# Identity products into spare columns of the y bank, behind the first FFN product

## Chip, cores and metric

One core of a Trainium2 chip runs the whole kernel in one launch. The metric is the device time of that launch in microseconds; the kernel before takes 502.52 us, the median of three runs (502.21 to 503.4).

## What is computed

A gated linear attention with a decay for each channel, and a feed-forward block on its output:

```python
for t in range(S):                                   # B, H, S, D = 4, 8, 768, 48
    state = alpha[:, :, t, :, None] * state + np.einsum('bhd,bhe->bhde', k[:, :, t], v[:, :, t])
    y[:, :, t] = np.einsum('bhd,bhde->bhe', q[:, :, t], state)
x = y.transpose(0, 2, 1, 3).reshape(B * S, H * D)    # 3072 x 384
h = x @ w_in                                         # 384 x 2048
out = (0.5 * h * (1.0 + erf(h / sqrt(2)))) @ w_out   # 2048 x 384
```

## The kernel before

The 3072 tokens are cut into 12 groups of 256 (`g`), and the eight heads of a group into two units (`u`), so there are 24 units; unit n is group n // 2. A unit passes through these steps:

- VectorE (DVE) scans the decays (L283, L304) and multiplies queries and keys by them (L299, L309).
- TensorE (PE) forms the `scores` (L325) into a PSUM tile `s`. DVE masks them into `ss` (L340), and ScalarE (ACT) copies the turned keys out of the same tile into `kn` (L334, `turned_out`).
- PE multiplies the masked scores with v (`inside`, L399) into `ybank`, and `kn` with v into the same tile (`sums`, L426; in the first two groups `running`, L367). DVE adds the sums up to the states (L454, `chain`), and PE adds the share of the earlier chunks to y (`outside_part`, L487).
- y is split into a high and a low part for the FFN: ACT casts y to the high part (L541, `x_high`), PE subtracts that from y in the bank (L550, `x_minus`), and ACT casts what is left to the low part (L556, `x_rest`). Some rows are then moved between partitions by DMAs that SP and ACT issue (L564, `spread`).

The FFN runs in steps (g, f) over eight pairs of 128 columns of `w_in`: 18 products of 256 columns into the PSUM tile `hp` (L572, `gemm1`), two Gelus on ACT (L593, L594), the low part by a subtraction (L603 on PE and L607 on ACT early on, L599 on DVE later), and 12 products into `acc` (L622, `gemm2`). The weights come as 64-bit floats and are turned into two 32-bit parts on DVE and ACT (L197 to L259) in the first 135 us, while the first groups are already being worked on.

`ybank` is one PSUM tile of two banks with 512 columns each. Columns 0 to 255 of a bank hold y and columns 256 to 447 hold the sums; columns 448 to 511 hold nothing.

The order on PE, DVE, ACT and SP is made in Python before anything is issued. A planner gives each step an assumed cost (`COST`, us) and a start; the steps sorted by planned start are then issued one by one under a manual schedule, so the planned start sets the order on each engine. What a step must wait for is found by the framework from what was issued before it, and is expressed as a semaphore count that the other engine has to reach.

Into planned gaps of PE before the first `gemm1` the plan puts `busy(n)`: n products of the identity with itself (L1080) into `spare`, a tile that nobody reads. A gap gives int((gap - 0.3) / 0.24) of them. A float32 product is two matmul instructions in the profile (42 rows for 21 products).

Of the kernel before, what the change touches and what calls it, by code (L numbers as in the profile page):

```python
# [25 lines left out]
WAIT = 0.15  # L26
SLOW = 1.1
FILL = 0.24
UNTIL = 60.0
SUMS = 2  # L30
LANES = 8
# [13 lines left out]
def gla_then_gelu_ffn(ctx: ExitStack, tc: tile.TileContext, q, k, v, alpha, akq, w_in, w_out, out):  # L45
    nc = tc.nc
    B, H, D, S = q.shape
# [3 lines left out]
    C = 128  # L51
# [24 lines left out]
    ident = const.tile([P, P], F32, name="ident")  # L76
# [20 lines left out]
    minus = const.tile([P, P], F32R, name="minus")  # L97
# [55 lines left out]
    ybank = ps_y.tile([P, 2, BANK], F32, name="ybank")  # L153
# [448 lines left out]
    def gelu_rest(g, f, hp, ghi):  # L602
        nc.tensor.matmul(hp, lhsT=minus, rhs=ghi, start=False, stop=True, skip_group_check=True)  # L603

        def out():
            glo = half_tile("glo", LO_GAP, g, f)
            nc.scalar.copy(glo, hp)  # L607
            return glo

        return out  # L610
# [313 lines left out]
    steps, plan, evacuated = [], [], set()  # L924
# [42 lines left out]
    def gemm1_op(g, t):  # L967
# [18 lines left out]

        if g < NSB and t < UNTIL:
            st["minus"] = Op("PE", "minus", lambda: st.update(rest=gelu_rest(g, f, st["hp"], st["gh"])), [st["gelu"]], rank=-3)
# [41 lines left out]
    def choose(e, t):  # L1030
        best = None
        for o in waiting[e]:
            at = when(o)
            if at is not None and at <= t + 1e-9 and (best is None or (o.rank, o.n) < (best.rank, best.n)):
                best = o
        if e != "PE":
            return best
        if best is not None and not (best.late and best.at() + MARGIN > t):
            return best
        held = best  # L1040
        second = [s for s in steps if s["gemm2"].start is None]
        if second:
            at = when(second[0]["gemm2"])
            if at is not None and at <= t + 1e-9:
                return second[0]["gemm2"]
        if len(second) < 2:
            hp_free = steps[-2]["low"].end if len(steps) > 1 else 0.0
            if hp_free is not None and hp_free + WAIT <= t + 1e-9 or len(steps) < 2:
                g = next_step(t)
                if g is not None:  # L1050
                    return gemm1_op(g, t)
        return held
# [3 lines left out]
    while True:  # L1056
        moved = False
        for e in ("DVE", "ACT", "PE", "SP", "POOL"):
            if free_at[e] <= t + 1e-9:
                o = choose(e, t)  # L1060
# [13 lines left out]
    plan.append(Op("DVE", "part", lambda: last["out"](), [last["gemm2"]]))  # L1074
    plan[-1].start = t + 10
    spare = ps_h.tile([P, 2, G], F32, tag="hp", name="spare")[:, 0, :P]

    def busy(n):
        for _ in range(n):
            nc.tensor.matmul(spare, lhsT=ident, rhs=ident, start=True, stop=True)  # L1080

    first = min(o.start for o in plan if o.name == "gemm1")
    early = sorted((o for o in plan if o.eng == "PE" and o.start <= first), key=lambda o: o.start)
    for o, after in zip(early, early[1:]):
        n = int((after.start - o.end - 0.3) / FILL)
        if n > 0:
            plan.append(Op("PE", "minus", lambda n=n: busy(n)))
            plan[-1].start = o.start + 0.01
    plan.sort(key=lambda o: (o.start, o.n))

# [72 lines left out]
```

## Time and profile before

| what | value |
|---|---|
| median of three runs (lowest, highest) | 502.52 us (502.21, 503.4) |
| profiled execution, its own time | 503.02 us |
| its span, first to last instruction | 501.0 us |
| PE busy / weight loads | 487.1 us (97%) / 474.9 us (95%) |
| DVE busy | 301.7 us (60%) |
| ACT busy | 217.9 us (43%) |
| mean granted TensorE clock | 0.995 |

The profiled execution took 2.02 us more than its span, and 0.50 us more than the median of the runs. Busy shares are means over the span: DVE is busy nearly without a break in the first 135 us and a quarter of the time behind that.

### The profile page before, as it was taken

What the parts mean: (1) busy time and instruction counts of PE and PEld (TensorE: products, weight loads), DVE (VectorE), ACT (ScalarE), POOL (GpSimd) and SP (SyncE); (2) the same over time, 40 slices, a digit from 0 to 9 for tenths busy, and PEclk for the clock granted to TensorE, in tenths of its full rate; (3) what the DMA queues carried; (4) which work ended last, traced back from release to release, by engine and by line L of the source; (5) the groups of instructions that cost most, each with busy time, mean ns of one, the idle gap of its engine ahead of it and who ended that gap; (6) DMA issues with size and microseconds to landing.
All of it is one profiled execution on the core that took longest, in us unless ns stands there. A gap on an engine that the chain in (4) does not pass through costs nothing.

```text
span 501.0 us, 13833 instructions
## 1 busy us (share of the span) xinstructions
PE 487.1 (97%) x5970; PEld 474.9 (95%) x5970; DVE 301.7 (60%) x580; ACT 217.9 (43%) x467; POOL 34.8 (7%) x69
## 2 busy tenths in 40 slices
PE   7898999999999999999999999999999999999996
PEld 7777899999998999998999999999999999999996
DVE  6999999999789999899266264251232211211211
ACT  2776856645445555555352352351332222222221
POOL 4100011000111121211010011000000000000000
PEclk9998999999999999999999999999999999999999
DMA  8967363531024453344031020010010000000001
GB/s 299 391 189 236 123 234 128 188 128 65 0 89 147 139 170 120 103 163 143 1 86 60 2 82 2 0 49 2 1 46 4 0 33 1 33 0 1 33 0 37
DMA packets 17153, 44.20 MB, mean 88 GB/s; under 512 B 2240, under 2 KB 8512, under 8 KB 17088
## 3 DMA queue, kind: packets, MB, share of 16 engines
q1 hardware_dynamic: 16656, 42.87, 25.3%
q8 instruction: 49, 0.80, 0.7%
q10 hardware_dynamic: 432, 0.39, 0.3%
q14 instruction: 16, 0.13, 0.1%
HBM read 36.18 MB, written 4.72 MB: 82 GB/s over the span
## 4 chain that ended last, share of the span: by engine, by line
PE 85%; DVE 9%; issue 2%; ACT 1%; DMA 1%; SPq 0%; DVEq 0%
PE acc L622 38%; PE hp L572 38%; PE s L325 3%; PE ybank L399 2%; PE ybank L487 2%; DVE rp L304 2%; DVE pp L283 2%; PE ybank L426 2%; DMA akq<-in_akq_dram 1%; DVE qk L299 1%; DVE ss L340 1%; DVE x L545 1%; DVE glo L599 1%; DVE akq L309 0%; DVE states L454 0%
## 5 line engine op out<-in xcount | busy, mean ns | idle before, releaser
L572 PE MATMUL hp<-x,wih 128*128 128x256 f32 x1152 | 202.5, 278 | 0.0
L572 PEld LDWEIGHTS hp<-x,wih 128*128 128x128 f32 x1152 | 179.2, 189 | 0.6
L572 PE MATMUL hp<-x,wil 128*128 128x256 f32 x576 | 159.8, 278 | 0.0
L599 DVE TENSOR_TENSOR glo<-hp,ghi 128x512 fp32r<-128x512 f32 x92 | 63.1, 686 | 160.4 <-ACT hp L594 160.3
L593 ACT ACTIVATE ghi<-hp 128x512 fp32r<-128x512 f32 x96 | 57.4, 598 | 197.7 <-PE hp L572 197.4
L622 PE MATMUL acc<-woh,ghi 128*128 128x384 f32 x384 | 130.9, 341 | 0.0
L622 PE MATMUL acc<-wol,ghi 128*128 128x384 f32 x384 | 128.9, 336 | 0.0
L572 PEld LDWEIGHTS hp<-x,wil 128*128 128x128 f32 x576 | 108.9, 189 | 0.0
L622 PE MATMUL acc<-woh,glo 128*128 128x384 f32 x384 | 82.5, 335 | 2.0 <-DVE glo L599 2.0
L622 PEld LDWEIGHTS acc<-woh,ghi 128*128 128x128 f32 x384 | 72.1, 188 | 1.7
L622 PEld LDWEIGHTS acc<-wol,ghi 128*128 128x128 f32 x384 | 72.1, 188 | 0.0
L622 PEld LDWEIGHTS acc<-woh,glo 128*128 128x128 f32 x384 | 67.8, 188 | 2.8 <-DVE glo L599 2.7
L594 ACT ACTIVATE hp<-hp 128x512 f32<-128x512 f32 x96 | 56.9, 593 | 0.0
L304 DVE TENSOR_TENSOR_SCAN rp<-akq,rp,top 128x255 f32<-128x255 f32 x48 | 35.8, 774 | 0.8
L283 DVE TENSOR_TENSOR_SCAN pp<-akq,top 128x256 f32<-128x256 f32 x48 | 31.0, 679 | 3.9 <-POOL qk L299 2.0
L299 POOL TENSOR_TENSOR qk<-akq,pp 128x512 f32<-128x512 f32 x18 | 24.8, 1380 | 45.8 <-DVE pp L283 15.5
L325 PE MATMUL s<-qk,akq 48*64 48x112 f32 x768 | 23.9, 260 | 2.3 <-DVE akq L309 1.1
L541 ACT CAST x<-ybank 64x256 fp32r<-64x256 f32 (+4 forms) x60 | 20.0, 333 | 9.4 <-PE ybank L487 5.0
L334 ACT COPY kn<-s 128x384 f32<-128x384 f32 x24 | 11.5, 480 | 28.9 <-DVE ss L340 16.3
L454 DVE TENSOR_TENSOR states<-ybank,states 128x96 f32<-128x96 f32 x66 | 16.8, 255 | 10.1 <-ACT x L541 7.8
L309 DVE TENSOR_TENSOR akq<-akq,rp 128x512 f32<-128x512 f32 x24 | 22.2, 926 | 0.7
L325 PEld LDWEIGHTS s<-qk,akq 48*64 48x64 f32 x768 | 19.3, 133 | 3.2 <-issue 1.5
(79 smaller groups left out, 390.3 us busy)
## 6 DMA issues: line engine op xcount, KB each, us to landing
akq<-in_akq_dram SPq DMA_DIRECT2D x22, 768.0 KB, 5.2
st<-in_moe_w_in_dram SPq DMA_DIRECT2D x8, 768.0 KB, 4.4
st<-in_moe_w_out_dram SPq DMA_DIRECT2D x8, 768.0 KB, 4.9
vn<-in_v_dram SPq DMA_DIRECT2D x12, 384.0 KB, 4.9
out_dram<-part SPq DMA_DIRECT2D x11, 384.0 KB, 3.0
x<-z SPq DMA_DIRECT2D x63, 32.0 KB, 1.9
akq<-in_akq_dram SPq DMA_DIRECT2D x2, 512.0 KB, 5.2
akq<-in_akq_dram SPq DMA_DIRECT2D x2, 256.0 KB, 4.5
```

The source lines that it names most:

```text
L283: nc.vector.tensor_tensor_scan(pp[:, i], at[:, i], top, MID, ALU.mult, ALU.min)
L299: eng.tensor_tensor(out=qs[:, :, :, :CS], in0=by_chunk(qt), in1=by_chunk(pp), op=ALU.mult)
L304: nc.vector.tensor_tensor_scan(rp[:, i, G - 2 :: -1], at[:, i, G - 1 : 0 : -1], top[:, 1:], rp[:, i, G - 1 :], ALU.mult, ALU.min)
L309: nc.vector.tensor_tensor(out=kt, in0=kt, in1=rp, op=ALU.mult)
L325: nc.tensor.matmul(d["s"][o, h, e : e + KW], lhsT=d["kt"][r, i, t], rhs=d["qs"][r, i, j], start=True, stop=True)
L454: d["chain"] = nc.vector.tensor_tensor(out=st[j + 1], in0=new, in1=st[j], op=ALU.add)
L541: nc.scalar.copy(hi, y)
L572: nc.tensor.matmul(hp[:, j, :], lhsT=a[:, j, i * P : (i + 1) * P], rhs=x[:, i, :], start=(j == 0 and i == 0 and n == 0), stop=(i == NK - 1 ...
L593: nc.scalar.activation(ghi, hp, AF.Gelu)
L594: nc.scalar.activation(hp, hp, AF.Gelu)
L599: nc.vector.tensor_tensor(out=glo, in0=hp, in1=ghi.bitcast(F32), op=ALU.subtract)
L622: nc.tensor.matmul(acc[t], lhsT=a[:, j, t * C : (t + 1) * C], rhs=w[:, j, :], start=(first and j == 0 and k == 0 and w is wo_hi[f]), stop= ...
```

## The change

Gaps of the plan are now filled up to a planned start of 80 us and no longer only up to the first `gemm1`. Behind the first `gemm1` a gap must leave 0.8 us over, in place of 0.3, and the products go into columns 448 to 511 of bank 1 of `ybank`, 64 columns wide and without the start flag, in place of `spare`, which shares its slots with `hp`.

```diff
+WARM_UNTIL, WARM_REST = 80.0, 0.8
...
     spare = ps_h.tile([P, 2, G], F32, tag="hp", name="spare")[:, 0, :P]
-
-    def busy(n):
+    margin = ybank[:, 1, 2 * C + 4 * D :]
+
+    def busy(n, to, anew):
         for _ in range(n):
-            nc.tensor.matmul(spare, lhsT=ident, rhs=ident, start=True, stop=True)
+            nc.tensor.matmul(
+                to, lhsT=ident, rhs=ident[:, : to.shape[1]], start=anew, stop=True, skip_group_check=not anew
+            )
 
     first = min(o.start for o in plan if o.name == "gemm1")
-    early = sorted((o for o in plan if o.eng == "PE" and o.start <= first), key=lambda o: o.start)
+    early = sorted((o for o in plan if o.eng == "PE" and o.start <= WARM_UNTIL), key=lambda o: o.start)
     for o, after in zip(early, early[1:]):
-        n = int((after.start - o.end - 0.3) / FILL)
+        anew = after.start <= first
+        n = int((after.start - o.end - (0.3 if anew else WARM_REST)) / FILL)
         if n > 0:
-            plan.append(Op("PE", "minus", lambda n=n: busy(n)))
+            plan.append(Op("PE", "minus", lambda n=n, anew=anew: busy(n, spare if anew else margin, anew)))
             plan[-1].start = o.start + 0.01
```

The whole program gains seven products, in two places; nothing else changes its order on any engine. Lines are numbered one higher in the changed kernel up to the fill, so L325 is L326 there.

The first place is PE between the scores of unit 4 (`s_0_709`) and `inside` of the same unit. Before:

```order
L550 MATMUL ybank<-z_695,minus 128x128 x2
L550 MATMUL ybank<-x_557,minus 128x128 x2
L325 MATMUL s_0_709<-qk_120,akq_117 64x112 x16
L399 MATMUL ybank<-ss_0_736,vn_116 64x64 x16
L426 MATMUL ybank<-vn_116,kn 64x48 x12
```

With the change:

```order
L551 MATMUL ybank<-z_695,minus 128x128 x2
L551 MATMUL ybank<-x_557,minus 128x128 x2
L326 MATMUL s_0_709<-qk_120,akq_117 64x112 x16
L1082 MATMUL ybank<-ident 128x64 x6
L400 MATMUL ybank<-ss_0_742,vn_116 64x64 x16
L427 MATMUL ybank<-vn_116,kn 64x48 x12
```

Six products stand between the scores and `inside`. They are issued before the casts of `x_rest` of unit 3, which the plan starts later than the scores. On ACT the order around these casts is the same as before (`z_695` and `x_557` are where unit 3's low part goes):

```order
L557 CAST z_695<-ybank 128x256 [waits PE_49]
L557 CAST x_557<-ybank 128x256
L565 DMA x_557<-z_695 16x512 [waits Activation_49]
L565 DMA x_557<-z_695 16x512 [waits DMAHW5_49]
L565 DMA x_557<-z_695 16x512 [waits DMAHW7_49,Activation_49]
L335 COPY kn<-s_0_709 128x384 [waits DVE_49]
```

The rows are the same; the count of PE's semaphore that the first cast waits for is not. Before it is 352, which PE reaches with the last subtraction of unit 3; the scores bring it to 368. In the changed program it is 374, which PE reaches with the sixth identity product.

The second place is PE between the subtractions of unit 4 and the Gelu subtraction of step (1, 0), with the change:

```order
L604 MATMUL hp_1_784<-ghi_1_831,minus 128x512
L551 MATMUL ybank<-x_856,minus 128x256 x2
L1082 MATMUL ybank<-ident 128x64
L604 MATMUL hp_0_835<-ghi_0_866,minus 128x512
```

One product stands there, and the `x_rest` cast of unit 4 waits for it in the same way.

## Rows read from the trace of the kernel before

**Rows 1.** The page, part 1 and the chain that ended last by engine.
```profile
PE 487.1 (97%) x5970; PEld 474.9 (95%) x5970; DVE 301.7 (60%) x580; ACT 217.9 (43%) x467; POOL 34.8 (7%) x69
...
PE 85%; DVE 9%; issue 2%; ACT 1%; DMA 1%; SPq 0%; DVEq 0%
```

**Rows 2.** Windows: stretch, length, busy us (count) of engines, PEclk, DMA share, GB/s.
```profile
20.00:25.00 5.00, 4.01 (x86) 3.56 (x86) 4.82 (x9) 2.78 (x10) 1.43 (x4) 1.00 0.99 364
45.00:50.00 5.00, 5.00 (x68) 4.71 (x62) 4.83 (x10) 3.57 (x8) 0.21 (x1) 0.66 0.60 190
60.00:500.00 440.00, 434.72 (x5087) 427.75 (x5087) 248.11 (x493) 181.32 (x389) 27.63 (x38) 1.00 0.20 65
```

**Rows 3.** The quarter of a microsecond in which the clock falls.
```profile
45.75:46.00 0.25, 0.25 (x3) 0.25 (x2) 0.25 (x1) 0.05 (x1) 0.00 (x0) 0.62 0.04 8
```

**Rows 4.** Timeline of PE: start, us, line, out<-in, shape, count [idle before <-releaser].
```profile
9.79 1.38 PE L1080 MATMUL spare<-ident 128*128 128x128 f32 x10
...
23.05 1.00 PE L325 MATMUL s<-qk,akq 48*64 48x112 f32 x32 [0.99 <-PE ybank L487]
...
41.96 1.00 PE L325 MATMUL s<-qk,akq 48*64 48x112 f32 x32
44.46 0.69 PE L399 MATMUL ybank<-ss,vn 64*64 64x64 f32 x32 [1.50 <-issue]
45.12 0.67 PE L426 MATMUL ybank<-vn,kn 64*64 64x48 f32 x24
45.72 0.74 PE L572 MATMUL hp<-x,wih 128*128 128x256 f32 x2
...
49.56 1.10 PE L487 MATMUL ybank<-qk,states 48*48 48x64 f32 x32
...
54.15 0.50 PE L603 MATMUL hp<-ghi,minus 128*128 128x512 f32 x1 [0.70 <-ACT hp L594]
...
56.67 1.00 PE L325 MATMUL s<-qk,akq 48*64 48x112 f32 x32
```

**Rows 5.** The chain that ended last, in order of time: start, us, what.
```profile
45.79 3.85 PE hp L572 x18
...
64.59 2.32 PE hp L572 x18
```

**Rows 6.** Timeline of ACT; ACTq is a DMA issue that holds ACT's queue.
```profile
42.07 0.37 ACT L556 CAST z<-ybank 128x256 fp32r<-128x256 f32 x1 [0.30 <-PE ybank L550]
42.34 0.38 ACT L556 CAST x<-ybank 128x256 fp32r<-128x256 f32 x1
42.47 2.07 ACTq L564 DMA_DIRECT2D x<-z  x3
44.59 0.48 ACT L334 COPY kn<-s 128x384 f32<-128x384 f32 x1 [1.87 <-DVE ss L340]
...
54.50 0.60 ACT L556 CAST x<-ybank 128x512 fp32r<-128x512 f32 x1
```

**Rows 7.** Timeline of PE's weight loads.
```profile
41.37 0.30 PEld L550 LDWEIGHTS ybank<-z,minus 128*128 128x128 f32 x2
41.59 0.30 PEld L550 LDWEIGHTS ybank<-x,minus 128*128 128x128 f32 x2
```

**Rows 8.** Timeline of DVE.
```profile
43.68 0.68 DVE L340 TENSOR_TENSOR ss<-s,mask 128x512 f32<-128x512 f32 x1
...
47.32 0.81 DVE L454 TENSOR_TENSOR states<-ybank,states 128x96 f32<-128x96 f32 x3
...
54.66 0.69 DVE L309 TENSOR_TENSOR akq<-akq,rp 128x512 f32<-128x512 f32 x1
```

**Rows 9.** Timeline of SP's queue.
```profile
42.47 1.78 SPq L564 DMA_DIRECT2D x<-z  x3
46.25 0.37 SPq L197 DMA_DIRECT2D st<-in_moe_w_in_dram  x1
```

**Rows 10.** The page, DMA issues: count, KB each, median us to landing.
```profile
x<-z SPq DMA_DIRECT2D x63, 32.0 KB, 1.9
```

## The prediction

> **What bounds the kernel now.** The page comes first: PE is busy 97% of the span and carries 85% of the chain that ended last, DVE 9% [rows 1]. So a microsecond that PE loses or gains is worth close to a microsecond, if nothing else holds PE later. The windows come next, read for PEclk. It is 1.00 (2.4 GHz) from 60 to 500 us, and 0.66 in the mean from 45 to 50 [rows 2]. At the two levels 1.00 and 0.50 a mean of 0.66 is 5 x 0.34 / 0.5 = 3.4 us at half clock, 1.2 GHz; the quarter from 45.75 has a mean between the levels, so the fall lies there [rows 3]. PE's timeline then tells what PE did before it: the scores of unit 4 start at 41.96 and end at 42.96, PE idles 1.50 us, and L399 and L426 run from 44.46 [rows 4]. An idle time of 0.99 us, at 22 to 23 us, left the clock at 1.00 [rows 4, 2]. The chain gives the price of the half clock: 18 products of L572 take 3.85 us there, and 2.32 where they stand at full clock behind the same kind of small products, 1.53 us less [rows 5].
>
> PE's idle time itself ends with DVE: the mask L340 starts at 43.68 and ends at 44.36, and L399 needs it [rows 8, 4].
>
> **The six products.** What does one cost? Each is two instructions with a full load of 128x128 weights. Ten instructions of L1080 with 128 moving columns take 1.38 us, 0.138 each with the last one's drain [rows 4]; that is the upper end. Half the columns might halve it, to 0.07, the lower end. But L550's weight loads come in pairs that start 0.22 us apart, 0.11 each [rows 7], though its 128 columns take one instruction and not two. There the load sets the pace, and 64 columns keep the same load, so I take 0.11: 12 x 0.11 = 1.32 us, from 42.96 to 44.28. By the ends it is 43.80 or 44.62. On PE alone this fits ahead of 44.46, or costs 0.16 us at the upper end.
>
> **The wait that they bring.** The products write bank 1 of `ybank`, and the low-part cast of unit 3 reads y from both banks. It is issued behind the products, and its semaphore count is now the one that the sixth product reaches (374 in place of 352). Before, it started at 42.07, right behind the subtraction [rows 6]; now it starts at 44.28, **2.21 us later** (1.73 to 2.55 by the ends above). Queued behind it on ACT, in order: the second cast (42.34, ends 42.72), three DMA issues that hold ACT from 42.47 to 44.54, and the copy of `kn`, which started at 44.59, right behind them [rows 6]. None has slack, as the copy was not waiting for the mask (44.36) but for the queue. So `kn` starts at 44.59 + 2.21 = 46.80.
>
> Who waits for that? L399 needs the second cast, since it overwrites y: 42.72 + 2.21 = 44.93, so it starts at about 45.0, 0.5 late. L426 needs `kn`: it started at 45.12, and starts at 47.33, after 1.6 us of new idle time. L572 follows at 47.93. The end of the scores to the start of L572 was 45.72 - 42.96 = 2.76 us, and becomes 4.97. **The gap that was to be filled is moved behind the products, not closed.**
>
> The Trainium skill (PSUM — Partial Sum Buffer, "PSUM bank collisions raise a hardware error") has a rule on this: two engines must not touch one bank in the same partitions at once, whichever columns they touch, so accesses are to be guarded by bank. By that rule the wait is due, and the time is the forecast below; were columns enough, no wait would be due, and the time would be the second rival's. No row of the kernel before shows it, as its scores go to another tile than y.
>
> **Other queues.** SP's three x<-z issues move from 42.47 to 44.68 and end at 46.46, so the weight fetch behind them moves from 46.25 by 0.2 [rows 9]; it serves a conversion some us later. The last x<-z issue of ACT ends at 46.75 and lands 1.9 later [rows 10], at 48.65; its reader, the first product of step (1, 0), stands behind L487 (49.56 to 50.6, and later now). Both are hidden. DVE's L454 starts at 47.32 and needs L426, so it waits until 47.93 and ends 0.6 us later than before; L487, which needs it, stood 1.4 us behind its end (48.13 against 49.56) [rows 8, 4]. So DVE's delay is hidden by PE's own. The **seventh product** stands ahead of L603, where PE idles 0.70 until 54.15 [rows 4]; it takes 0.22. The cast that now waits for it starts at 54.50 [rows 6], so it costs nothing; with that cover gone it would cost 0.22.
>
> **The sum.** L572 of step (0, 1) starts 2.21 us later. Whether the clock falls again then decides. I take it that it does: PE idles from about 44.3 to 45.0 and from 45.7 to 47.3, over 2 us in 3, where 1.50 us were enough before. The fall came 1.3 us after the idle time had ended (44.46 to 45.75); 1.3 after 47.33 is 48.6, with most of L572 still to come. It costs at most the 1.53 of before; part of the slow stretch may lie on L487, for which no row at half clock exists, and on its slack, so I bound it by 0.8 and 1.53 and take 1.2. Of the old fall, 1.53 goes. So +2.21 - 1.53 + 1.2 = +1.9 us, and the profiled execution's 503.02 becomes 504.9. It stood 0.50 above the median of the runs, so the forecast against that is **504.4 us**, 0.37% slower. Its own range: 1.73 - 1.53 + 0.8 = +1.0 to 2.55 - 1.53 + 1.53 = +2.55, 503.5 to 505.1; the 0.3 by which the lowest run of before lies under its median, added above, makes 505.4.
>
> **Rivals.**
> First, the clock stays at 1.00. For it: the products keep PE at work until 44.3, and each of the two idle times is not far above 0.99, which did no harm. Against it: they nearly touch. Then +2.21 - 1.53 = +0.7 us (0.2 to 1.0): 503.2. The Trainium skill (TensorE: Matmul & The Clock Gate, "Why this matters for your kernels") warns only of idle gaps longer than any of these; by its rule no fall would come, and none should have come in the kernel before, where rows 3 show one behind 1.50 us.
>
> Second, the fill works: the cast is not held, or its delay is hidden, the 1.50 us are filled, and the clock does not fall. It ends on the other side, faster. The price is not the whole 1.53: L487 can move up 1.4 until DVE's L454 holds it, and L325 at 56.67 stands 1.32 behind the end of DVE's L309 (55.35) [rows 4, 8], and DVE has no idle time there. So at most -1.27, 501.3. It decides if the cast starts before 42.5. The semaphore count speaks against it.
>
> Third, worse: the runs of before lie 1.19 us apart, and if the fall is missing in most of them, nothing comes back: +2.21 + 1.2 on 502.5 is 505.9. The Trainium skill (same page, "The HAM clock gate") says that the point at which the clock changes differs from run to run; no row here shows that.
>
> **Chances.** Clock falls again 0.62; clock stays 0.22; fill works 0.09; worse 0.07. A measurement of this kernel can tell 0.3% (1.5 us) from no change, so faster means under 501.0 and slower over 504.0. Faster: the lower third of the second rival, 0.03. Within: the rest of it 0.06, nearly all of the first 0.20, and 0.14 of the likeliest case, from its lower part: 0.40. Slower: the rest, 0.57. The range from 502.6 to 505.4 leaves out the second rival, most of the third, and little of the first at its lower end: under 0.2.
>
> **What would show it.** Right: six products in 1.2 to 1.5 us behind the scores, the cast of L557 at about 44.3, `kn` (L335) at about 46.8, L427 at about 47.3 behind a new idle time of PE with ACT as its releaser, and a stretch at 0.50 soon after. Wrong: the cast still at 42.1 and L427 at 45.1 (the count means something else), or PEclk at 1.00 from 45 to 55 (first rival), or products twice as fast as taken, which moves all by 0.5 us.

## The result, and the profile after

The change makes the kernel **slower by 0.71%**: 506.43 us in the median of 10 runs (505.23 to 507.8) against 503.01 for the kernel before in the same sessions (10 runs, 501.86 to 505.47), ratio 1.0071, 95% interval 1.0059 to 1.0083. The forecast was 504.4 with a range to 505.4: the right side, and too small. The profiled execution took 507.0 us with a span of 504.9, against 503.02 and 501.0 before.

The page first, busy time and the chain by engine, which answer to [rows 1]:

```profile
PE 490.5 (97%) x5984; PEld 478.1 (95%) x5984; DVE 302.1 (60%) x580; ACT 217.8 (43%) x467; POOL 35.1 (7%) x69
...
PE 87%; DVE 7%; issue 2%; ACT 2%; ACTq 1%; DMA 1%; SPq 0%; DVEq 0%
```

PE gains 14 instructions and 3.4 us of busy time, 1.5 us more than those 14 take (1.55 + 0.33 in the timeline below): other products have become slower. Where, the windows tell (columns as in [rows 2]):

```profile
45.00:50.00 5.00, 2.95 (x62) 2.72 (x63) 3.52 (x8) 3.06 (x8) 0.21 (x1) 0.66 0.34 74
50.00:55.00 5.00, 5.00 (x53) 4.70 (x53) 4.86 (x9) 2.59 (x6) 0.00 (x0) 0.66 0.75 283
60.00:500.00 440.00, 437.96 (x5137) 430.78 (x5136) 250.95 (x497) 183.77 (x394) 27.61 (x38) 1.00 0.20 64
```

From 45 to 50 us PE is busy for 2.95 us in place of 5.00 [rows 2]. Two neighbouring stretches now have a mean of 0.66, where before there was one: 2 x 5 x 0.34 / 0.5 = 6.8 us at 1.2 GHz, twice the 3.4 of before. PE's timeline over the same place, to be laid beside [rows 4]:

```profile
42.14 1.00 PE L326 MATMUL s<-qk,akq 48*64 48x112 f32 x32
43.07 1.55 PE L1082 MATMUL ybank<-ident 128*128 128x64 f32 x12
45.35 0.69 PE L400 MATMUL ybank<-ss,vn 64*64 64x64 f32 x32 [0.74 <-ACT x L557]
...
47.74 1.09 PE L427 MATMUL ybank<-vn,kn 64*64 64x48 f32 x24 [1.69 <-ACT kn L335]
...
52.90 1.31 PE L488 MATMUL ybank<-qk,states 48*48 48x64 f32 x32
...
56.84 0.33 PE L1082 MATMUL ybank<-ident 128*128 128x64 f32 x2
57.71 0.50 PE L604 MATMUL hp<-ghi,minus 128*128 128x512 f32 x1 [0.54 <-ACT hp L595]
...
60.25 1.00 PE L326 MATMUL s<-qk,akq 48*64 48x112 f32 x32
...
77.09 1.00 PE L326 MATMUL s<-qk,akq 48*64 48x112 f32 x32
```

The one idle time of 1.50 us has become two, 0.74 and 1.69 us, both ended by ACT. ACT's timeline says why; it answers to [rows 6]:

```profile
44.66 0.37 ACT L557 CAST z<-ybank 128x256 fp32r<-128x256 f32 x1 [2.70 <-PE ybank L1082]
44.92 0.38 ACT L557 CAST x<-ybank 128x256 fp32r<-128x256 f32 x1
45.06 2.11 ACTq L565 DMA_DIRECT2D x<-z  x3
47.21 0.48 ACT L335 COPY kn<-s 128x384 f32<-128x384 f32 x1 [1.91 <-DVE wol L260]
```

ACT idles 2.70 us before the cast, which the identity products release. The releaser printed for the copy of `kn` is a DVE instruction, but what stands right in front of it is the DMA issues that hold ACT's queue until 47.17. The chain that ended last prices the slow stretch, beside [rows 5]:

```profile
47.74 1.09 PE ybank L427 x24
48.83 4.14 PE hp L573 x18
52.97 1.24 PE ybank L488 x32
54.21 2.33 PE hp L573 x18
```

Of the trace alone, in the forecast's own terms (start times of the same instruction in both traces):

| term | forecast | measured |
|---|---|---|
| scores of unit 4 later (a difference of the two executions that arises ahead of the products) | 0 | +0.18 |
| cast held, so L427 later | +2.21 (1.73 to 2.55) | 47.74 - 45.12 - 0.18 = +2.44 |
| old fall of the clock goes | -1.53 | -1.53 |
| clock falls again | +1.2 (0.8 to 1.53) | L427 1.09 - 0.67, L573 4.14 - 2.32, L488 1.31 - 1.10: +2.45 |
| sum | +1.9 | +3.54 |

The scores of unit 5 start at 60.25 in place of 56.67, 3.58 us later, and those of unit 6 at 77.09 in place of 73.51, again 3.58. So the loss is complete at unit 5. Some 0.3 us more come much later, in two steps between 157 and 167 us and between 228 and 252 us; what makes them is left open.

### The profile page after: what moved, and what is told of

Its sections match the earlier page's. It is cut to its first block, busy times and chain, and to the rows that moved or that the text cites. A ratio compares the mean times of both kernels' runs of the same rounds, so it can differ in the third digit from the quotient of the medians.

```text
span 504.9 us, 13861 instructions
## 1 busy us (share of the span) xinstructions
PE 490.5 (97%) x5984; PEld 478.1 (95%) x5984; DVE 302.1 (60%) x580; ACT 217.8 (43%) x467; POOL 35.1 (7%) x69
## 4 chain that ended last, share of the span: by engine, by line
PE 87%; DVE 7%; issue 2%; ACT 2%; ACTq 1%; DMA 1%; SPq 0%; DVEq 0%
PE acc L623 38%; PE hp L573 38%; PE s L326 3%; PE ybank L488 2%; PE ybank L400 2%; PE ybank L427 2%; DVE rp L305 1%; DVE pp L284 1%; ACTq L565 1%; DMA akq<-in_akq_dram 1%; PE ybank L368 1%; DVE x L546 1%; DVE glo L600 1%; DVE ss L341 0%; DVE states L455 0%
## 5 line engine op out<-in xcount | busy, mean ns | idle before, releaser
L573 PE MATMUL hp<-x,wih 128*128 128x256 f32 x1152 | 203.1, 279 | 0.0
L573 PEld LDWEIGHTS hp<-x,wih 128*128 128x128 f32 x1152 | 179.4, 189 | 0.7
L573 PE MATMUL hp<-x,wil 128*128 128x256 f32 x576 | 160.1, 278 | 0.0
L573 PEld LDWEIGHTS hp<-x,wil 128*128 128x128 f32 x576 | 109.2, 190 | 0.0
L326 PE MATMUL s<-qk,akq 48*64 48x112 f32 x768 | 23.9, 260 | 1.3 <-PE ybank L488 0.9
L455 DVE TENSOR_TENSOR states<-ybank,states 128x96 f32<-128x96 f32 x66 | 16.8, 255 | 11.4 <-ACT x L542 7.8
L310 DVE TENSOR_TENSOR akq<-akq,rp 128x512 f32<-128x512 f32 x24 | 22.2, 927 | 0.7
L326 PEld LDWEIGHTS s<-qk,akq 48*64 48x64 f32 x768 | 19.3, 133 | 2.2 <-PE ybank L488 1.0
```

The costliest lines, as they stand in the source:

```text
L310: nc.vector.tensor_tensor(out=kt, in0=kt, in1=rp, op=ALU.mult)
L326: nc.tensor.matmul(d["s"][o, h, e : e + KW], lhsT=d["kt"][r, i, t], rhs=d["qs"][r, i, j], start=True, stop=True)
L455: d["chain"] = nc.vector.tensor_tensor(out=st[j + 1], in0=new, in1=st[j], op=ALU.add)
L573: nc.tensor.matmul(hp[:, j, :], lhsT=a[:, j, i * P : (i + 1) * P], rhs=x[:, i, :], start=(j == 0 and i == 0 and n == 0), stop=(i == NK - 1 ...
```

## Experiments

Each kernel ran in five rounds beside the kernel before; in these sessions that took 503.2, 503.14 and 503.17 us.

**1. The products behind the cast.** The same products go at the end of the gap and not at its start, so the cast is issued ahead of them.

```diff
-            plan[-1].start = o.start + 0.01
+            plan[-1].start = o.start + 0.01 if anew else after.start - 0.01
```

> The six products stay where they are on TensorE, but are issued behind the low-part cast instead of ahead of it, so that they wait for the cast and the cast does not wait for them. Theory A (the wait on the products holds ACT's queue, and all else follows): the cast starts near 42.1, the copy of kn near 44.6, the sums near 45.2, the idle time of 1.5 us is filled; the clock stays at 1.00 there, and the kernel is 0 to 1.3 us faster than before, some 4 us faster than the change. Theory B (the products themselves cost, by their place on TensorE or by writing that bank): slower than before by about as much as the change, +2 to +3.5 us.

Measured: 502.73 us (501.68 to 504.77, 12 runs), ratio 0.9988 (0.9976 to 0.9999). The profiled execution, PE's timeline, then ACT's, then the window:

```profile
42.60 1.55 PE L1082 MATMUL ybank<-ident 128*128 128x64 f32 x12
44.13 0.69 PE L400 MATMUL ybank<-ss,vn 64*64 64x64 f32 x32
44.82 0.67 PE L427 MATMUL ybank<-vn,kn 64*64 64x48 f32 x24
...
55.21 1.00 PE L326 MATMUL s<-qk,akq 48*64 48x112 f32 x32 [0.19 <-DVE akq L310]
...
74.23 0.47 PE L573 MATMUL hp<-x,wih 128*128 128x256 f32 x2 [1.24 <-issue]
```

```profile
41.78 0.37 ACT L557 CAST z<-ybank 128x256 fp32r<-128x256 f32 x1 [0.29 <-PE ybank L551]
```

```profile
45.00:50.00 5.00, 4.84 (x83) 4.51 (x80) 4.86 (x10) 4.49 (x10) 0.21 (x1) 1.00 0.69 198
```

The wait is gone with the order alone; number, shape and target of the products are those of the change. The 1.50 us are filled without a break, the clock stays at 1.00, and at the scores of unit 5 PE is 1.46 us ahead of the kernel before. Of these, 0.29 were there at the scores of unit 4 (41.67 against 41.96), ahead of the products; the other 1.17 are the gain, and DVE's L310 holds PE from more. At 74 us that gain is lost in one wait of 1.24 us. That became experiment 6.

**2. The same place, another bank.** The products stand where the change puts them, and write 64 spare columns of a tile of `acc`, widened to a whole bank (the lines that widen it are left out).

```diff
...
-            plan.append(Op("PE", "minus", lambda n=n, anew=anew: busy(n, spare if anew else margin, anew)))
+            plan.append(Op("PE", "minus", lambda n=n, anew=anew: busy(n, spare if anew else spare_cols[1][:, DM : DM + 64], anew)))
```

> Same place in the order as in the change, but the products go to spare columns of the second acc bank (its tile made 512 columns wide) instead of the y bank. Theory A: no cast reads that bank, so the first cast's count is 352 again and it starts near 42.1; time as in the run with the products behind the cast, 0 to 1.3 us faster than before. Theory B (the place in the order costs): as slow as the change, +3 us. If only the y bank's write costs, this one and the run before it differ by over 2 us.

Measured: 503.28 us (501.83 to 504.1, 12 runs), ratio 0.9994 (0.9982 to 1.0006). PE, then ACT:

```profile
42.49 1.55 PE L1084 MATMUL acc<-ident 128*128 128x64 f32 x12
```

```profile
41.67 0.37 ACT L557 CAST z<-ybank 128x256 fp32r<-128x256 f32 x1 [0.30 <-PE ybank L551]
```

The cast starts before the products. So neither their place nor their time holds it, but that they write the tile that it reads, though no column of it that it reads. Bank and tile change together here, so the run does not tell which of the two sets the wait. As in experiment 1 the lead, 1.57 us of which 0.40 were there ahead of the products, is lost at 74 us.

**3. One product in place of six**, in the first place alone.

```diff
+        if not anew:
+            n = 1 if n > 1 else 0
```

> One product in place of six at the first place, none at the second. Theory A: the cast waits for the scores (42.96) and the one product, so it starts near 43.4, 1.3 us late instead of 2.6, and kn and the sums move by the same 1.3; the clock falls as in both kernels, for once or twice 3.4 us. So slower than before by 1 to 2.5 us, with one sixth of the products. Theory B: the cost goes with the number of products: one sixth of 3.5, 0.6 us at most.

Measured: 505.09 us (502.76 to 506.08, 11 runs), ratio 1.0028 (1.0015 to 1.0042). PE's timeline, then the windows:

```profile
43.30 0.43 PE L1082 MATMUL ybank<-ident 128*128 128x64 f32 x2
44.87 0.88 PE L400 MATMUL ybank<-ss,vn 64*64 64x64 f32 x32 [1.13 <-ACT x L557]
46.88 1.09 PE L427 MATMUL ybank<-vn,kn 64*64 64x48 f32 x24 [1.14 <-ACT kn L335]
```

```profile
45.00:45.50 0.50, 0.50 (x32) 0.50 (x30) 0.50 (x1) 0.00 (x0) 0.00 (x0) 0.73 0.39 117
45.00:50.00 5.00, 3.86 (x66) 3.58 (x65) 4.58 (x9) 3.52 (x7) 0.21 (x1) 0.52 0.48 132
50.00:55.00 5.00, 5.00 (x58) 4.70 (x58) 4.90 (x9) 2.36 (x4) 0.00 (x0) 0.79 0.74 251
```

Counted from the scores of unit 4, which start at 42.38 here, one product makes L427 1.34 us late, against 2.44 with six. Most of the wait with one product is for the scores, which PE does before it: they end 0.89 us behind the old start of the cast (42.96 against 42.07), and the cast is 1.29 us late (it starts at 43.78). Two idle times of 1.13 and 1.14 us again stand beside some 6.9 us at half clock, 5 x 0.48 / 0.5 + 5 x 0.21 / 0.5. But the fall comes behind the first alone: the mean of 0.73 from 45.0 to 45.5 puts it at about 45.23, while PE is at work on L400.

**4. The second gap filled as well.** The change, and six more products of the same kind between L400 and the sums of unit 4, so that the wait stays and PE idles little.

```diff
+        if (g, u) == (2, 0):
+            for _ in range(6):
+                nc.tensor.matmul(
+                    ybank[:, 1, 2 * C + 4 * D :], lhsT=ident, rhs=ident[:, :64], start=False, stop=True, skip_group_check=True
+                )
```

> The change, and six more products in the new idle time between the masked products with v and the sums (1.7 us). The wait on ACT stays: cast near 44.6, sums near 47.7. Theory A1 (of the loss, 2.4 us is the wait and the rest is the longer time at half clock, which comes from the idle time): PEclk stays at 1.00 from 45 to 55, products of L572 take 2.3 us instead of 4.1, and the kernel is only 0.5 to 1.2 us slower than before. Theory A2 (the clock falls for another reason, the added products included): slow stretch as in the change, 3 to 4 us slower than before.

Measured: 504.87 us (504.04 to 507.81, 12 runs), ratio 1.0039 (1.0024 to 1.0054). PE, then the windows:

```profile
43.08 1.55 PE L1087 MATMUL ybank<-ident 128*128 128x64 f32 x12
45.37 0.69 PE L400 MATMUL ybank<-ss,vn 64*64 64x64 f32 x32 [0.74 <-ACT x L562]
45.99 1.55 PE L410 MATMUL ybank<-ident 128*128 128x64 f32 x12
47.78 0.67 PE L432 MATMUL ybank<-vn,kn 64*64 64x48 f32 x24 [0.24 <-ACT kn L335]
```

```profile
45.00:50.00 5.00, 4.39 (x82) 4.14 (x83) 3.90 (x9) 3.03 (x8) 0.21 (x1) 1.00 0.53 135
50.00:55.00 5.00, 4.69 (x62) 4.30 (x60) 4.89 (x8) 4.02 (x8) 0.00 (x0) 1.00 0.69 224
```

The sums are as late as in the change (47.78 against 47.74), and the clock does not fall in the profiled execution (7 of the 12 runs have a mean of 0.997 or more, none of the change's). This parts the loss, roughly: 504.87 - 503.2 = 1.7 us for the wait, more than the 0.5 to 1.2 expected, and 506.43 - 504.87 = 1.6 us for the fall of the clock, across sessions and with both kinds of runs in each median but the change's. By the profiled executions the fall weighs more: the scores of unit 5 start at 57.73 here and at 60.25 in the change, 2.5 us apart. This kernel's profiled execution was one of its quicker runs (504.19).

**5. The seventh product alone.**

```diff
-        if n > 0:
+        if n > 0 and (anew or n == 1):
```

> The change with the six products behind the scores of unit 4 left out and the seventh, behind the first x_minus before the products of minus, kept. Theory: no engine has to wait longer for it, the first cast starts at 42.1 as before, and the fall of the clock at 45.8 is as in the kernel before: ratio 0.998 to 1.002. Rival: part of the 0.71% comes from the seventh product, whose bank the casts of the next x_rest read: ratio 1.002 to 1.004.

Measured: 502.71 us (501.74 to 504.14, 11 runs), ratio 0.9993 (0.9981 to 1.0004): it costs nothing. Its profiled execution shows something else. PE's timeline at the two places, and the window:

```profile
44.63 0.69 PE L400 MATMUL ybank<-ss,vn 64*64 64x64 f32 x32 [1.50 <-issue]
...
74.31 0.47 PE L573 MATMUL hp<-x,wih 128*128 128x256 f32 x2 [0.87 <-PE s L326]
```

```profile
45.00:50.00 5.00, 4.84 (x102) 4.42 (x94) 4.83 (x10) 4.50 (x10) 0.21 (x1) 1.00 0.62 185
```

The same 1.50 us of idle time as in the kernel before, the same products around it, and here the clock did not fall. **The fall of the kernel before is not in every execution.** Of its 86 runs beside these experiments 34 had a mean granted clock of 0.997 or more. The mean does not say where the clock was low, and 3.4 us at half clock lower it by 3.4 x 0.5 / 501 = 0.0034, to 0.997 at best: five of the 34 stand at 0.997 and may have the fall, 29 stand higher. In the three sessions the 34 took 503.10, 503.00 and 503.12 us in the median, the others 503.25, 503.24 and 503.25: the fall cost 0.1 to 0.2 us at the end (up to 0.3 with the line drawn above 0.997), not 1.53. The second row says where the rest stays: this execution, without the fall, is 1.01 us ahead at the scores of unit 5, and only 0.13 us ahead after the wait at 74 us. Counted from the scores of unit 4 the 1.01 are 1.17, as many as in experiments 1 and 2 with the gap filled. So in an execution that keeps its clock anyway the products gained nothing here.

**6. What PE waits for at 74 us.** These are the first products on x of group 2; they need its six x<-z transfers. In experiment 1 SP issues a weight fetch of 768 KB at 67.21, between the first and the other five. Here experiment 1 stands with that fetch behind SP's three.

```diff
+    for get in [o for o in plan if o.name == "fetch"]:
+        for o in plan:
+            if o.name == "spread" and o.eng == "SP" and 0 < o.start - get.start < 1.5 and get.start > 5:
+                get.start = o.start + 0.001
```

> The products behind the cast, as in e1_behind_cast, and in addition SP issues the one weight fetch (768 KB, issued at 67.21 there) behind its three x<-z transfers of group 2 instead of ahead of them. Theory: in e1_behind_cast the 1.46 us won by 56.67 were lost at the first products of hp at 74.4 because the x<-z transfers, though issued 1.1 to 1.5 us earlier, landed no earlier (74.66 against 74.41), being queued behind that fetch. Then they land 1.5 to 3 us earlier here, no wait of over 0.3 us stands before those products, and of the 1.46 us at least 1.0 is still there at 75 us and in most part at the end: about 501.7 us against 503.2 before, ratio 0.995 to 0.998. Rival: the transfers are held by the load of alpha, k and q (768 KB, landing until 69.83) and by their own small pieces, not by the fetch: landing within 0.5 us of 74.66 and the ratio of e1_behind_cast, 0.998 to 1.000. A second rival: the late fetch delays the conversion that needs it and a wait for weights takes the place of the wait for x: ratio 1.000 or above.

Measured: **501.69 us** (501.3 to 503.53, 12 runs), ratio 0.9973 (0.9964 to 0.9983). The view of DMA issues from 66 to 75 us (count, KB each, median us to landing) for experiment 1:

```profile
x<-z ACTq DMA_DIRECT2D x3, 32.0 KB, 6.2
x<-z SPq DMA_DIRECT2D x3, 32.0 KB, 6.3
```

And for this kernel, with PE's timeline behind it:

```profile
x<-z SPq DMA_DIRECT2D x3, 32.0 KB, 2.6
x<-z ACTq DMA_DIRECT2D x3, 32.0 KB, 2.8
```

```profile
72.06 1.00 PE L326 MATMUL s<-qk,akq 48*64 48x112 f32 x32
72.99 0.50 PE L573 MATMUL hp<-x,wih 128*128 128x256 f32 x2
```

In experiment 1 the last transfer landed at 74.66, in the kernel before, which issues them 1.1 to 1.5 us later, at 74.41, and here at 70.63. The wait is gone, the lead is 1.45 us behind it, and the span is 1.4 us shorter than before.

**7. The fetch alone.** The same four lines in the kernel before, without products, in two sessions.

> The kernel before with no product added, and SP's one weight fetch (issued at 68.43) behind its three x<-z transfers of group 2. By the theory that the landing of x costs something only once the steps ahead of it are early, this gains nothing by itself: the x<-z transfers land 1 to 3 us earlier than 74.41, the products of hp start at 74.4 as before, ratio 0.998 to 1.002. Rival: the landing had already held something in the kernel before, and the edit alone gives what e5_late_fetch gives, ratio 0.995 to 0.998; then the gain of e5_late_fetch would have nothing to do with the products behind the cast.

> The kernel of e6_fetch_only once more, beside e8_bank_and_fetch on one chip, for the comparison of the two. Theory: about 502.3, granted clock 0.997 or above in about half of the executions, and those near 501.6, the others near 502.8. Rival: no such split; then the clock of this stretch doesn't set the difference.

Measured: 502.27 us (501.46 to 505.2, 12 runs), ratio 0.9983 (0.997 to 0.9996), and then 502.75 (501.24 to 503.83, 12 runs), 0.999 (0.9977 to 1.0003). This half refutes the expectation that it gains nothing: the runs part by the clock as the second text says. In the first session the six at 0.997 or more took 501.64 in the median and the other six 502.83; in the second five took 501.67 and seven 503.02. With x early, an execution that keeps its clock keeps the 1.2 to 1.4 us too. The profiled execution of the second session is one: counted from the scores of unit 4 it is 1.31 us ahead of the kernel before at the scores of the last unit, and experiment 6, with products, 1.28.

**8. Another bank and the fetch.** Experiment 2 with the same four lines.

> The change with its products in spare columns of the accumulator's bank (as in e2_other_bank) and the one weight fetch behind the x<-z issues of group 2 (as in e5_late_fetch). Theory: both losses are gone, the wait of the cast and the wait for x, so this comes out as e5_late_fetch did: ratio 0.996 to 0.998, granted clock 0.997 or above in at least 9 of 12 executions. Beside e9_fetch_again it tells whether the products add anything to the moved fetch: by the theory they keep the clock up in executions in which it falls otherwise, so the median lies 0.3 to 0.8 us under that of e9_fetch_again. Rival: the moved fetch alone gives the gain, and the medians lie within 0.2 us of each other.

Measured: 502.35 us (501.54 to 503.63, 12 runs), ratio 0.9984 (0.9972 to 0.9995); 8 of 12 at 0.997 or more, one short of what was expected. In the profiled execution the clock falls too, at another place; PE's timeline and the windows:

```profile
30.18 1.10 PE L488 MATMUL ybank<-qk,states 48*48 48x64 f32 x32 [1.32 <-ACT states L446]
```

```profile
30.00:35.00 5.00, 4.78 (x50) 4.51 (x51) 4.38 (x8) 4.27 (x10) 0.21 (x1) 0.69 0.70 193
...
45.00:50.00 5.00, 4.93 (x106) 4.54 (x107) 4.86 (x9) 4.16 (x9) 0.21 (x1) 1.00 0.63 195
```

It is whole at the filled place and 0.69 from 30 to 35 us, behind an idle time of 1.32 us at 29 us that nothing fills. In the change the idle time there was 1.38 us, and the clock stayed at 1.00:

```profile
30.14 1.10 PE L488 MATMUL ybank<-qk,states 48*48 48x64 f32 x32 [1.38 <-ACT states L446]
```

```profile
30.00:35.00 5.00, 4.82 (x60) 4.46 (x60) 4.32 (x8) 4.63 (x11) 0.21 (x1) 1.00 0.64 199
```

Against the moved fetch alone in the same session the products are worth 502.75 - 502.35 = 0.40 us, and 502.27 - 501.69 = 0.58 in the session of experiment 6. Runs at 0.997 or more: 18 of 24 with products, 11 of 24 without. Over both sessions the 95% interval of the difference of the medians, drawn anew from the runs, reaches from 0.95 us in their favour to 0.43 against. So that well placed products add something to the moved fetch is likely, and not shown. What is shown is that they keep the clock up more often: over all sessions 39 of the 48 runs with the gap filled and no wait added (experiments 1, 2, 6 and 8) have 0.997 or more, and 53 of the 121 with the gap open (the kernel before and experiments 5 and 7); above 0.997 it is 38 and 46.

## Why the forecast was too low

**The wait: right.** The semaphore count meant what it was read to mean. The cast stood at 44.66 (forecast 44.28), `kn` at 47.21 (46.80), L427 at 47.74 (47.33) with ACT as releaser, L400 at 45.35 (45.0). Experiments 1 to 3 show the cause from three sides: order, bank, and a single product. The Trainium skill's rule (PSUM — Partial Sum Buffer, "PSUM bank collisions raise a hardware error"), to guard by bank and not by columns, agrees with the 2.70 us of the change against the 0.30 of experiment 2. The runs show that the wait goes with the write, whichever columns it takes; whether bank or tile sets it, and what two engines in one bank would do without it, no run shows.

**The price of a product: at the upper end.** 1.55 us for twelve instructions, against 1.32 taken and 1.66 as the bound. That is the +0.23 in the second row of the table. Halving the columns from 128 to 64 took the price only from 0.138 to 0.13 each.

**The step that failed: "the clock falls again, cost bounded 0.8 to 1.53, taken 1.2".** That it would fall was right, and all 10 runs of the change have a clock under 0.997. The size was taken from the one fall in the trace of before, as if a fall had one length. With two idle times close together the low stretch was twice as long, here and in experiment 3. It began while PE still waited for `kn`, where the forecast had expected 48.6: the half microsecond from 46.50 has a mean of 0.56, 0.5 x 0.44 / 0.5 = 0.44 us at half clock, so it fell at about 46.56.

```profile
46.50:47.00 0.50, 0.00 (x0) 0.00 (x0) 0.50 (x2) 0.00 (x0) 0.00 (x0) 0.56 0.71 144
```

So it caught L427, all 18 products of L573 (4.14, more than the 3.85 that had served as the ceiling) and L488, 2.45 us. This alone is 1.25 of the missing 1.64 us. The upper bound was no bound: it came from an execution in which the fall set in part of the way, and left out the case that all of the stretch is slow. Experiment 4 supports the price, 2.5 us between the profiled executions; why the stretch was longer is argued from two traces and not shown.

**The credit for the old fall and the base.** The 1.53 us hold, and the sum needs them: without them 503.01 + 2.44 + 2.45 would be 507.9. They do not depend on the fall being in the run that one compares with, as a run of before that keeps its clock gives its lead back at x of group 2 (experiment 5), while in the change the delay of 3.58 us stood unchanged behind that place. Between medians the change is 506.43 - 503.01 = 3.42 us slower, close to the 3.54 of the trace. So of the 2.03 us by which the forecast was too low, 0.49 are the base (three runs, 502.52, where 503.01 was measured beside the change) and about 1.5 the sum. The third rival, that nothing comes back, gave 505.9 and had 0.07; it came nearest, by luck. Its condition, no fall in *most* runs, was not met, and its sum leaves out a credit that was due and takes 1.2 for a fall that cost 2.45.

**The other rivals.** First, the clock stays: it did not, but experiment 4 is this case made, +1.17 us from profile to profile (0.19 of it ahead of the products) where +0.7 (0.2 to 1.0) was worked out. The Trainium skill (TensorE: Matmul & The Clock Gate, "Why this matters for your kernels") warns of longer idle gaps only. The traces disagree: the clock fell behind 1.50 us, behind 1.13 us (experiment 3), and inside the second of two idle times of 0.74 and 1.69 us. The Trainium skill's other statement (same page, "The HAM clock gate") is that the point of change differs from run to run. Here not only when the fall comes differs but whether it comes, with 34 of 86 runs of the kernel before at 0.997 or more. Second, the fill works: experiment 1 is this case. Of the 1.27 us worked out (the prediction has 1.32 and then 1.27, without the step between) 1.17 were there at the scores of unit 5, with DVE's L310 as the limit that it had named; at the end none were left (503.08 against 503.02 in the profiled executions). With the fetch moved as well, experiment 6, it is -1.36 us from profile to profile. What the forecast had missed is the landing of x behind it. It took 1.9 us for an x<-z from the page's median [rows 10], where the view of these issues in the kernel before has 4.5 to 4.8:

```profile
x<-z ACTq DMA_DIRECT2D x3, 32.0 KB, 4.8
x<-z SPq DMA_DIRECT2D x3, 32.0 KB, 4.5
```

**The hidden parts: right.** The seventh product cost nothing. DVE's L455 waited 1.38 us for L427, more than the 0.6 forecast, and L488 still did not wait for it.

## What to carry to other kernels

Filler for an idle engine is not free because nobody reads its result: look at what it makes others wait for, by tile and bank, and issue it behind the reads of that bank that are due, or into a bank that nobody reads then. Before a gap is filled, follow the gain to the next wait: here it was given back 20 us later, at small transfers behind a large one, and reordering that fetch alone gained as much as the fill alone or more (0.87 and 0.42 us in two sessions, against 0.47 in experiment 1 and nothing in experiment 2). And a price read off one slow stretch of one execution is a sample and not a bound.

## What the runs showed of the hardware

- With the same 1.50 us of idle time the clock fell in one profiled execution and stayed in another, and at 29 us it stayed behind 1.38 us and fell behind 1.32; of the falls that came while TensorE was at work, the one behind the shortest idle time followed 1.13 us (experiment 3). Of 86 runs of the kernel before, 34 have a mean of 0.997 or more. Beside two idle times close together (0.74 and 1.69, or 1.13 and 1.14 us) the clock was low for some 6.8 us, and 1 of 21 runs has such a mean.
- The clock can fall while TensorE idles, here 1.2 us before the next product (46.56 against 47.74), which then starts slow.
- An x<-z transfer of 32 KB took 1.9 us in the page's median. In the median of three it took 6.2 to 6.3 with a weight fetch of 768 KB ahead of most and the load of another 768 KB under way, and 2.6 to 2.8 with the fetch behind them. ACT's transfers suffered as much as SP's, though SP issued the fetch.
